# Attention in three blocks an element in place of six, between the products of an MLP mixer

## The chip, the cores and the metric

One core of one Trainium2 chip runs the whole program. The metric is device time in microseconds (us) of one execution; the kernel before took 1268.9 us (median of three runs, 1266.23 to 1271.95).

## The reference

Attention over normalised queries and keys, then an MLP mixer on its output, all in float32. There are 8 elements (batch), 12 heads, 448 positions and 64 numbers a head; the mixer has a width of 768, 256 token features and 1536 channel features.

```
q_n, k_n = rmsnorm(q) * g_q, rmsnorm(k) * g_k        # over the 64 numbers of a head
scores = q_n @ k_n.T / sqrt(64)                      # 448 x 448 for each head
attn   = exp(scores - max); attn /= sum(attn) + 1e-9
x      = (attn @ v), heads side by side              # 8 x 448 x 768
u      = x + (relu(x.T @ w_tok1) @ w_tok2).T         # mixing over positions
out    = u + relu(u @ w_ch1) @ w_ch2                 # mixing over channels
```

## The kernel before, in words

Everything is laid out by hand: within `manual_schedule` each engine runs its instructions in the order in which Python issues them, and semaphores hold an instruction until its operands and its buffer are ready. SP issues nearly all DMAs, also in that order.

**Heads and pairs.** Two heads make a pair `p` (48 in all, six an element), two pairs make a step `t` (24 in all, three an element). Attention of a step consists of seven scores (`score(t, k)`, L459: four quarter-array matmuls of 64x64 weights against 448 columns, then two exponentials on ACT, L463, into a tile `e`), seven value columns (`values(pair, k)`, L532, into the two banks `o_ps` of `ps_O`), the sums of the seven `e` tiles on DVE (`group_sums`, L500, six adds into `es`), and `row_sums` (L512), which multiplies `es` by ones into two tiles `d_ps`. `denominators` then takes for each pair the transpose of `d_ps` on DVE (L561) and its reciprocal (L563), in `begin`, and in `end` the transposed reciprocal (L575) and the product with `o_ps` (L578) into `uT`, the attention's output.

**Norms.** The queries and keys of a pair are squared on ACT (`square`, into the one tile `sq`), reduced on DVE (`reduce`, L1549), folded by four small copies on ACT (L1557), rooted by a first guess on DVE (L1571) and three Newton steps of four instructions on POOL (L1579 to L1582), scaled on DVE (`scale`, L1600) and transposed on DVE (`turn_qk`, L436), with a scaling on ACT for one of the two (L439). Only then can the pair's scores be taken. The next pairs' q and k are loaded into the same two tiles afterwards (L1514).

**Mixing.** Elements are mixed one after the other while attention is taken one element ahead. For an element `b` from 2 on the mixing is: `tok1` (L850, L857); `tok2` (L977), or for elements 3 to 6 the seven products of `seven_items` (L936); sums of the moving operand (`moving_sums`, L998 to L1002); 21 products of `ch1` (three groups of seven, L1097, twelve matmuls as the profile counts them), whose results are combined through `r` tiles by ACT, DVE and POOL (L1103, L1107, L1119) into `hb`; and 15 products of `ch2` in two halves each (L1163, eight matmuls a half), combined by L1178. Both halves of a `ch2` product go into one PSUM bank, as do the two halves of one output of `plain_2`, which stands for `ch2` in element 1. Further sums within `hb` (`x_form`, L1137) make the operands of the next `ch2` products.

**PSUM.** The eight banks are split: `ps_S` has four (scores, `d_ps`, some `tok1`), `ps_O` two, `ps_M` two (`m_tile()`: all the mixing's products). A tile gets a bank of its pool that is free by then, and its first matmul waits for the bank's last reader.

**Blocks.** From step `BIG` (9) on, a step's attention matmuls are issued in two blocks: `first_block` (scores 0 and 1, the step before's last values, its row sums, score 2) and `second_block` (scores 3 and 4, values 0 to 3, scores 5 and 6). `BLOCKS` names the places of the six blocks of an element among its mixing products (0 to 20 are `ch1`, 21 to 50 the halves of `ch2`), and `place` puts each block there and spreads the DVE, ACT and POOL items that belong behind it (`between`) evenly over the products up to the next block. Element 1 has one block, the first half of step 9, put by `merge` among `plain_2`.

Of the kernel before, what the change touches and what calls it, by code (L numbers as in the profile page):

```python
# [83 lines left out]
def whole(ctx, tc, shifted, pre, q, k, v, g_q, g_k, moe_w_tok1, moe_w_tok2, moe_w_ch1, moe_w_ch2, out):  # L84


    nc = tc.nc
# [10 lines left out]
    NPAIR = H // 2  # L98
# [15 lines left out]
    NM = S // P  # L114
    assert S - NM * P == D and NM == NS - 1 and NJ == 2

    UNITS = 8
    WCOLS = 512

# [287 lines left out]

    def load_v(p):
        b, hs = heads(p)
        st["v", p] = vt = pre.v_0 if p == 0 else st["v45"][:, p - 4, :] if p in (4, 5) else pre.v_t[p % 3]  # L410
# [129 lines left out]
    def row_sums(t):  # L540
        es = st.pop(("es", t))
        for p in (2 * t, 2 * t + 1):
            st["d", p] = s_tile("d_ps")
            ones(p, es[:, p % 2, :], start=True, stop=True)

    def denominators(ps):

        def begin(p):
            b, j = divmod(p, NPAIR)
            if j == 0:  # L550
                st["uT", b] = uT_pool.tile([P, NC, S], F32, name="uT")
# [9 lines left out]
            nc.vector.transpose(out=dt[:], in_=src)  # L561
            st["rc", p] = rc = pre.nt_pool.tile([P, NB], F32, name="rc")
            nc.vector.reciprocal(out=rc[:], in_=dt[:].rearrange("p (n c) -> p n c", c=32)[:, :, 0])  # L563

        def raw(p):

            b, j = divmod(p, NPAIR)
            to = st["uT", b][:, j, :]
            nc.scalar.copy(out=to, in_=st["o", p][:, 0:S])
            st["o", p] = to  # L570

        def end(p):
            b, j = divmod(p, NPAIR)
# [12 lines left out]
    BIG = NPAIR + NPAIR // 2  # L586

    def big_step(t, second):

        p, n = 2 * t, 2 * t + 2  # L590
        pair, last, live, more = (p, p + 1), (p - 2, p - 1), p < NP, 2 * t + 2 < NP
        item = lambda fn, *a, c=0.4: (c, lambda: fn(*a))
        loads = lambda j: [(0.3, fn) for fn in pre.loads(j, st, nc.sync, nc.sync)] if j < NP else []

        def first_block():
            if live:
                score(t, 0)
                score(t, 1)
            if more and t > BIG:
                pre.reduce(n, st)  # L600
                pre.square(n + 1, st)
            for k in range(NK - 2 - (t > BIG), NK):
# [4 lines left out]
            if live:  # L607
                score(t, 2)

        def second_block():  # L610
            score(t, 3)
            score(t, 4)
            for k in range(4):
                values(pair, k)
            score(t, 5)
            score(t, 6)
            for i in pair:
                st.pop(("qkT", i))

        if not second:  # L620
            squares = [item(fn, i, st) for i in (n, n + 1) for fn in (pre.square, pre.reduce)] if more else []
            ahead, beside = (squares[:1], squares[3:]) if t > BIG else ([], [])
            between = [item(group_sums, t, k) for k in (1, 2) if live]
            ends, roots = ([(0.4, fn) for fn in fns] for fns in (denominators(last), pre.roots(n, st) if more else []))
            if t == BIG:
                return ahead, (5.4, first_block), beside, between + ends + [
                    item(load_v, i, c=0.0) for i in pair] + squares + roots
            between += roots[:1] + ends[:2] + roots[1:2]
            between += [it for both in zip(ends[2:], roots[2:4]) for it in both] if more else ends[2:]
            between += roots[4:] + [item(load_v, i, c=0.0) for i in pair if live]  # L630
            return ahead, (5.4, first_block), beside, between
        beside = [item(scale, n), item(scale, n + 1), item(turn_qk, n, 1), item(turn_qk, n, 0)] if more else []
        beside += [item(group_sums, t, k) for k in (3, 4)]
        between = [item(turn_qk, n + 1, 1), item(turn_qk, n + 1, 0)] + loads(n + 2) if more else []
        between += [item(group_sums, t, k) for k in (5, 6)] + loads(n + 3)
        return [], (6.2, second_block), beside, between

    def place(units, blocks, at, later_beside):

        res, i, rest = [], 0, []  # L640
        for j, (ahead, block, beside, between) in list(zip(at, blocks)) + [(len(units), ([], None, [], []))]:
            n, done = j - i, 0
            for m in range(n):
                if m == n - 1 and block:
                    res += ahead
                res.append(units[i + m])
                upto = -(-len(rest) * (m + 1) // n)
                res += rest[done:upto]
                done = upto
            if not n:  # L650
                res += rest + ahead
            i, rest = j, between
            if block and later_beside and not j - at[0]:
                res.append(block)
                rest = beside + between
            elif block:
                res += [block] + beside
        return res

    def att_step(g):  # L660
# [95 lines left out]
            items.append((0.0, lambda: load_v(p + 1)))  # L756
        if live and s == 1 and 5 < p + 2 < NP:
            items.append((0.0, lambda: load_v(p + 2)))
        js = []
        if live and s == 0:  # L760
            js = [n, n + 1] if pre.plain(p) else [n + 1]
# [466 lines left out]
    def x_items(b, h):  # L1228
        return [(0.1, lambda j=j: trans_x(b, j)) for j in range(h * NC // 2, (h + 1) * NC // 2)]
# [113 lines left out]
    left, (some, sums) = [], sum_items()  # L1343
    for b in range(B):
        early, double = middle_items(b)
        if b == 0:
# [21 lines left out]
        att = []  # L1368
        if b + AHEAD < B and (shifted or b < 2):
            att = att_items(lo, lo + 10) + x_items(b + AHEAD, 0)  # L1370
            if shifted:
                att += att_items(lo + 10, lo + per)
            elif not b:
                step = att_step(lo + per - 1)
                att += att_items(lo + 10, lo + per - 1) + step[:5] + x_items(1, 1) + step[5:]
            else:
                run(att[:6])
                ahead, block, beside, between = big_step(BIG, False)
                att = att[6:] + att_items(lo + 10, lo + per - 1) + ahead + [block] + beside + between
        elif b + AHEAD < B:  # L1380
            t = (b + AHEAD) * NPAIR // 2
            blocks = [big_step(t + i // 2, i % 2) for i in range(1, NPAIR + 1)]
            blocks[4][3].extend(x_items(b + 1, 0))
            early = place(early, blocks, [near(early, at) for at in BLOCKS], in_seven(b))
        if b == 0:
            last = x_items(1, 1) * shifted + merge(last, sums[:5], turns(b, y_order(b)[2:4]))
        else:
            if b + 1 < B:
                last = merge(last, x_items(b + 1, 1))
            if b == 2 and not shifted:  # L1390
                last.append((0.4, right_sums))
            last += last_items(b, ends)
# [279 lines left out]
```

## Time and profile before

| | |
|---|---|
| runs, median (lowest to highest) | 1268.9 us (1266.23 to 1271.95) |
| profiled execution, its own time | 1268.99 us |
| its span | 1267.2 us |
| granted TensorE clock | 1.0 |
| busy: PE, PEld, DVE, ACT, POOL | 98%, 71%, 65%, 31%, 34% |
| one element of the steady part (3 to 6) | 146.90 us |
| DVE, ACT, POOL busy in such an element | 98.8, 46.2, 44.7 us |

PE is TensorE's matmuls, PEld its weight loads, DVE VectorE, ACT ScalarE, POOL GpSimd, SP the DMA-issuing engine. A line of a timeline gives start, duration, engine, source line, operation, output and inputs, shapes and the number of merged instructions; matmuls are pipelined, so the difference of two starts says what a stretch cost, and the duration is a little longer. A line of the groups gives the number of instructions after the x, then the busy time in us, the mean of one in ns and the idle time before them with what ended it. Each float32 matmul of the program is two in the profile.

### The profile page before, as it was taken

How to read it: one execution, taken by the hardware profiler on the slowest of the kernel's cores; microseconds unless marked ns; L12 is line 12 of the kernel's file. 1: busy time of each engine (PE TensorE's matmuls, PEld its weight loads, DVE VectorE, ACT ScalarE, POOL GpSimd, SP SyncE). 2: the span in 40 equal slices, each digit the busy share in tenths (PEclk: the TensorE clock that was granted, in tenths of full speed). 3: DMA queues.
4: the chain of work that ended last, by engine and by line, in shares of the span. 5: the costliest groups of instructions: out<-in, count | busy, mean ns of one | idle time of the engine just before them, and what ended most of it. 6: DMA issues, size and time to landing. Idle time of an engine off the chain costs nothing.

```text
span 1267.2 us, 20382 instructions
## 1 busy us (share of the span) xinstructions
PE 1244.7 (98%) x7322; PEld 903.5 (71%) x7322; DVE 827.8 (65%) x1293; ACT 397.1 (31%) x797; POOL 434.0 (34%) x674
## 2 busy tenths in 40 slices
PE   6999999999999999999999999999999999999998
PEld 3444444457745488798778877897787878797998
DVE  6988889756663455867677476766758486554243
ACT  6664433124330134402442143312343034300210
POOL 2311641044994912234224132244122342131222
PEclk9999999999999999999999999999999999999999
DMA  9666696899889786695758757684866865386554
GB/s 210 153 172 178 189 245 177 198 251 261 223 225 265 157 202 157 142 243 110 177 145 209 164 148 179 153 224 108 193 165 144 225 131 153 117 212 144 182 174 105
DMA packets 480274, 228.39 MB, mean 180 GB/s; under 512 B 362900, under 2 KB 440084, under 8 KB 480164
## 3 DMA queue, kind: packets, MB, share of 16 engines
q1 hardware_dynamic: 472626, 211.85, 66.9%
q0 software_dynamic: 4512, 14.46, 4.0%
q8 instruction: 60, 0.98, 0.3%
q10 hardware_dynamic: 3026, 0.69, 0.3%
q14 instruction: 50, 0.41, 0.1%
HBM read 184.26 MB, written 42.66 MB: 179 GB/s over the span
## 4 chain that ended last, share of the span: by engine, by line
PE 86%; DVE 5%; SPq 3%; DMA 2%; issue 1%; ACT 1%; POOL 1%; DVEq 0%; ACTq 0%; POOLq 0%
PE m_ps L1097 26%; PE m_ps L1163 22%; PE s_ps L459 10%; PE o_ps L532 9%; PE m_ps L1067 5%; PE m_ps L977 3%; PE m_ps L850 3%; PE t_ps L850 2%; PE m_ps L1146 1%; PE seven_ps L936 1%; PE d_ps L512 1%; PE m_ps L936 1%; PE m_ps L512 1%; DVE es L500 1%; DMA xs<-xt 1%
## 5 line engine op out<-in xcount | busy, mean ns | idle before, releaser
L1163 PEld LDWEIGHTS m_ps<-hb,unit 128*128 128x128 f32 x1440 | 270.9, 190 | 8.8 <-issue 7.7
L1163 PE MATMUL m_ps<-hb,unit 128*128 128x224 f32 x1440 | 277.2, 354 | 0.0
L1097 PE MATMUL m_ps<-tu,unit 128*128 128x224 f32 x1008 | 201.6, 355 | 1.3 <-ACT r L1107 1.3
L1097 PEld LDWEIGHTS m_ps<-tu,unit 128*128 128x128 f32 x1008 | 189.1, 190 | 15.0 <-issue 9.2
L463 ACT ACTIVATE e<-s_ps 128x448 f32<-128x448 f32 x294 | 138.3, 549 | 149.6 <-PE s_ps L459 148.9
L1097 PE MATMUL m_ps<-uT,unit 128*128 128x224 f32 x756 | 151.2, 354 | 0.6 <-DVE hb L1103 0.6
L1097 PEld LDWEIGHTS m_ps<-uT,unit 128*128 128x128 f32 x756 | 142.2, 190 | 7.7 <-POOL tu L1001 2.8
L459 PE MATMUL s_ps<-qkT 64*64 64x448 f32 x1260 | 144.3, 545 | 0.8 <-ACT x L832 0.8
L532 PE MATMUL o_ps<-e,v 64*64 64x448 f32 x1148 | 130.0, 538 | 0.0
L500 DVE TENSOR_TENSOR es<-es,e 128x896 f32<-128x896 f32 x90 | 102.9, 1143 | 11.0 <-ACT e L463 6.4
L1103 POOL TENSOR_TENSOR hb<-r,r 128x448 f32<-128x448 f32 x21 | 23.8, 1133 | 217.5 <-ACT r L1119 217.5
L1103 DVE TENSOR_TENSOR hb<-m_ps,r 128x448 f32<-128x448 f32 x63 | 39.1, 620 | 88.9 <-POOL r L1103 57.5
L459 PEld LDWEIGHTS s_ps<-qkT 64*64 64x64 f32 x1260 | 45.7, 132 | 67.9 <-issue 56.2
L1579 POOL TENSOR_TENSOR nt<-rs 128x56 f32<-128x56 f32 (+1 forms) x54 | 21.2, 393 | 201.8 <-DVE rs L1571 199.0
L532 PEld LDWEIGHTS o_ps<-e,v 64*64 64x64 f32 x1148 | 46.1, 133 | 61.9 <-issue 59.8
L1178 POOL TENSOR_TENSOR uT<-uT,r 128x448 f32<-128x448 f32 x42 | 51.4, 1241 | 78.2 <-DVE r L1178 46.6
L1104 ACT ACTIVATE hb<-hb 128x448 f32<-128x448 f32 x84 | 48.2, 575 | 90.5 <-DVE hb L1103 68.5
L1549 DVE TENSOR_REDUCE ms<-sq 128x28 f32<-128x896 f32 (+2 forms) x44 | 47.4, 1080 | 43.5 <-ACT sq L1536 36.3
L324 POOL TENSOR_TENSOR raw<-raw 128x128 f32<-128x128 f32 x128 | 65.4, 531 | 20.8 <-DMA raw<-wp 16.3
L1103 DVE TENSOR_TENSOR r<-m_ps,r 128x448 f32<-128x448 f32 x42 | 26.0, 618 | 55.2 <-PE m_ps L1097 55.2
L1174 ACT COPY r<-m_ps 128x448 f32<-128x448 f32 x24 | 12.8, 532 | 156.5 <-PE m_ps L1163 156.5
L1178 DVE TENSOR_TENSOR uT<-uT,m_ps 128x448 f32<-128x448 f32 x41 | 24.9, 619 | 54.8 <-PE m_ps L1163 54.8
(177 smaller groups left out, 1776.1 us busy)
## 6 DMA issues: line engine op xcount, KB each, us to landing
unit<-ws SPq DMA_DIRECT2D x267, 384.0 KB, 4.1
raw<-in_moe_w_ch_dram SPq DMA_DIRECT2D x72, 256.0 KB, 3.6
v<-in_v_dram SPq DMA_DIRECT2D x96, 112.0 KB, 3.6
out_dram<-turned SPq DMA_DIRECT2D x182, 56.0 KB, 2.0
xs<-xt SPq DMA_DIRECT2D x52, 168.0 KB, 4.5
qk_t<-in_q_dram SPq DMA_DIRECT2D x144, 56.0 KB, 3.5
qk_t<-in_k_dram SPq DMA_DIRECT2D x144, 56.0 KB, 3.4
x<-xs SPq DMA_DIRECT2D x39, 192.0 KB, 4.2
```

The costliest lines, as they stand in the source:

```text
L324: nc.gpsimd.tensor_tensor(out=at[o], in0=at[x], in1=at[y], op=ALU.add if op == "+" else ALU.subtract)
L459: nc.tensor.matmul(out=pss[i][rows_of(i, a), 0:S], lhsT=qkT[h, 1, k * D:(k + 1) * D], rhs=qkT[h, 0, :], start=True, stop=True)
L463: nc.scalar.activation(out=e[:, i, :], in_=pss[i][:, 0:S], func=AF.Exp)
L500: nc.vector.tensor_tensor(out=es[:], in0=(es if k > 1 else st["e", t, 0])[:], in1=st["e", t, k][:], op=ALU.add)
L532: nc.tensor.matmul(out=st["o", p][a * D:(a + 1) * D, 0:S], lhsT=vt[rows, k * D:(k + 1) * D], rhs=e[rows, :], **kw)
L850: nc.tensor.matmul(out=st["t1", h][jc][:, 0:HC], lhsT=w1_sb[:, c, jc * P:(jc + 1) * P], rhs=st["x", b, h][:, :, c, :], start=start and c = ...
L1067: nc.tensor.matmul(out=ps, lhsT=a[:, o + 2 * half, :], rhs=natural(half * KF + t) if wide else u[:, half * KC + t, :], start=(t == 0 and h ...
L1097: nc.tensor.matmul(out=ps[:, j * HS:(j + 1) * HS], lhsT=w[:, t, j, :], rhs=m, start=(t == 0), stop=(t == KC - 1))
L1103: add = lambda e, o, x, y: e.tensor_tensor(out=o, in0=x, in1=y, op=ALU.add)
L1104: relu = lambda name: put_off(lambda: nc.scalar.activation(out=h[name], in_=h[name], func=AF.Relu))
L1163: nc.tensor.matmul(out=ps[:, x * HS:(x + 1) * HS], lhsT=st["w"][:, tile_at % 6, :], rhs=hb[:, X_SLOT[f], i, :], start=(i == 0), stop=(i == 3))
L1178: e.tensor_tensor(out=get(out), in0=get(x_), in1=get(y), op=ALU.add if op == "+" else ALU.subtract)
```

## The change

Each step from 9 on has one block in place of two, and an element three in place of six. The block holds scores 0 and 1, the step before's last two value columns, its row sums, the first half of its endings (`begin` on DVE and, new for these pairs, a copy of `o_ps` to `uT` on ACT), and then a score and a value column in turn, with the group sums between them. `row_sums` takes its two tiles from `ps_M` in place of `ps_S`. Behind each block come the rest of the endings, the value loads, and the whole of the next pairs' norms, spread over the products up to the next block; behind an element's last block `norms` are spread over what is left of `early`, and `turned` is merged with the transposes of x in `last`. Four value tiles are used in turn, so that a step's two tiles can be loaded while the last step's are in use.

```
+    BIG = NPAIR + NPAIR // 2
 def load_v(p):
+        if p >= 2 * BIG and not shifted:
+            vt = (pre.v_0, pre.v_t[0])[p % 2] if p // 2 % 2 else pre.v_t[1 + p % 2]
 def row_sums(t):
-            st["d", p] = s_tile("d_ps")
+            st["d", p] = m_tile() if t >= BIG - 1 else s_tile("d_ps")
 def denominators(ps):
-        if ps[0] < NPAIR:
+        if ps[0] < NPAIR or ps[0] >= 2 * BIG - 2 and not shifted:
             parts += [lambda p=p: raw(p) for p in ps]
-    def big_step(t, second):
+    def big_step(t):
...
+        def block():
+            if live:
+                score(t, 0)
+                score(t, 1)
+            for k in (NK - 2, NK - 1):
                 values(last, k)
             row_sums(t - 1)
             for i in last:
                 st.pop(("v", i))
+            for part in ends[:4]:
+                part()
+            if not live:
+                return
+            group_sums(t, 1)
+            score(t, 2)
+            for k in range(3, NK):
+                values(pair, k - 3)
+                group_sums(t, k - 1)
+                score(t, k)
+            values(pair, NK - 3)
...
+        beside = [item(group_sums, t, NK - 1)] if live else []
+        ends_ = [(0.4, fn) for fn in ends[4:]]
+        if not more:
+            return (11.3 if live else 2.3, block), beside, ends_, [], []
+        norms = [item(fn, i, st) for i in (n, n + 1) for fn in (pre.square, pre.reduce)]
+        norms += [(0.4, fn) for fn in pre.roots(n, st)] + [nothing] * 4
+        turned = [item(scale, n), nothing, item(scale, n + 1), nothing, item(turn_qk, n, 1), item(turn_qk, n, 0)] + loads(n + 2)
+        turned += [item(turn_qk, n + 1, 1), item(turn_qk, n + 1, 0)] + loads(n + 3)
+        values_in = [item(load_v, i, c=0.0) for i in (n, n + 1)]
+        return (11.3, block), beside, ends_ + values_in, norms, turned
...
-    BLOCKS = (0, 6, 11, 17, 23, 31)
+    BLOCKS = (0, 14, 28)
...
+                block, beside, ends_, norms, turned = big_step(BIG)
+                att = att[6:] + att_items(lo + 10, lo + per - 1) + [block] + beside + ends_
+                carry = [(0.4, lambda: None)] * 14 + norms + turned
         elif b + AHEAD < B:
             t = (b + AHEAD) * NPAIR // 2
-            blocks = [big_step(t + i // 2, i % 2) for i in range(1, NPAIR + 1)]
-            blocks[4][3].extend(x_items(b + 1, 0))
-            early = place(early, blocks, [near(early, at) for at in BLOCKS], in_seven(b))
+            steps = [big_step(t + i) for i in range(1, NPAIR // 2 + 1)]
+            blocks = [(block, beside, ends_ + norms + turned) for block, beside, ends_, norms, turned in steps[:2]]
+            blocks[1][2].extend(x_items(b + 1, 0))
+            block, beside, ends_, norms, turned = steps[2]
+            blocks.append((block, beside, ends_ + norms))
+            early = place(early, blocks, [near(early, at) for at in ((8, 20, 30) if b == 2 else BLOCKS)], carry)
+            behind, carry = turned, []
...
-                last = merge(last, x_items(b + 1, 1))
+                last = merge(last, x_items(b + 1, 1) + behind)
```

More of the change, by code (lines that the diff above doesn't have):

```diff
@@ L409, in load_v @@
         b, hs = heads(p)
-        st["v", p] = vt = pre.v_0 if p == 0 else st["v45"][:, p - 4, :] if p in (4, 5) else pre.v_t[p % 3]
+        if p >= 2 * BIG and not shifted:
+            vt = (pre.v_0, pre.v_t[0])[p % 2] if p // 2 % 2 else pre.v_t[1 + p % 2]
+        else:
+            vt = pre.v_0 if p == 0 else st["v45"][:, p - 4, :] if p in (4, 5) else pre.v_t[p % 3]
+        st["v", p] = vt
         for a in range(2):
@@ L585, in whole @@
     NG = 2 * NP
-    BIG = NPAIR + NPAIR // 2
-    def big_step(t, second):
+    assert BIG % 2
+    def big_step(t):
         p, n = 2 * t, 2 * t + 2
@@ L592, in big_step, with some @@
         item = lambda fn, *a, c=0.4: (c, lambda: fn(*a))
-        loads = lambda j: [(0.3, fn) for fn in pre.loads(j, st, nc.sync, nc.sync)] if j < NP else []
-        def first_block():
+        nothing = (0.4, lambda: None)
+        loads = lambda j: [item(some, j, lo) for lo in (0, 4)] if j < NP else []
+        ends = denominators(last)
+        def some(j, lo):
+            for fn in pre.loads(j, st, nc.sync, nc.sync)[lo:lo + 4]:
+                fn()
+        def block():
             if live:
@@ L598, in first_block @@
                 score(t, 1)
[L599 to L602, printed above, removed]
+            for k in (NK - 2, NK - 1):
                 values(last, k)
@@ L606, in first_block @@
                 st.pop(("v", i))
[L607 to L616, printed above, removed]
+            for part in ends[:4]:
[8 more added lines that the diff above has]
+                score(t, k)
@@ L617, in second_block @@
+            values(pair, NK - 3)
             for i in pair:
                 st.pop(("qkT", i))
[L620 to L641, printed above, removed]
+        beside = [item(group_sums, t, NK - 1)] if live else []
@@ L642, in place @@
+        values_in = [item(load_v, i, c=0.0) for i in (n, n + 1)]
+        return (11.3, block), beside, ends_ + values_in, norms, turned
+    def place(units, blocks, at, rest):
+        res, i = [], 0
+        for j, (block, beside, between) in list(zip(at, blocks)) + [(len(units), (None, [], []))]:
             n, done = j - i, 0
             for m in range(n):
-                if m == n - 1 and block:
-                    res += ahead
                 res.append(units[i + m])
@@ L650, in place @@
             if not n:
-                res += rest + ahead
+                res += rest
             i, rest = j, between
[L653 to L656, printed above, removed]
+            if block:
                 res += [block] + beside
@@ L758, in att_step @@
             items.append((0.0, lambda: load_v(p + 2)))
+            if t == BIG - 1 and not shifted:
+                items.append((0.0, lambda: load_v(p + 3)))
         js = []
@@ L1342, in whole @@
         att_items(0, 8) + merge(att_items(8, AHEAD * per + 1), x_items(0, 0)), weight_items(0, BEFORE)))
-    left, (some, sums) = [], sum_items()
+    left, carry, (some, sums) = [], [], sum_items()
     for b in range(B):
@@ L1367, in whole @@
         lo = (b + AHEAD) * per + 1
-        att = []
+        att, behind = [], []
         if b + AHEAD < B and (shifted or b < 2):
@@ L1377, in whole @@
                 run(att[:6])
-                ahead, block, beside, between = big_step(BIG, False)
-                att = att[6:] + att_items(lo + 10, lo + per - 1) + ahead + [block] + beside + between
+                block, beside, ends_, norms, turned = big_step(BIG)
+                att = att[6:] + att_items(lo + 10, lo + per - 1) + [block] + beside + ends_
+                carry = [(0.4, lambda: None)] * 14 + norms + turned
         elif b + AHEAD < B:
             t = (b + AHEAD) * NPAIR // 2
-            blocks = [big_step(t + i // 2, i % 2) for i in range(1, NPAIR + 1)]
-            blocks[4][3].extend(x_items(b + 1, 0))
-            early = place(early, blocks, [near(early, at) for at in BLOCKS], in_seven(b))
+            steps = [big_step(t + i) for i in range(1, NPAIR // 2 + 1)]
[5 more added lines that the diff above has]
+            behind, carry = turned, []
         if b == 0:
```

## The prediction

> **What bounds the kernel now.** I read the page first, then PE's timeline over one element, then every engine's timeline where mixing passes from its first to its second product stage, then the groups by shape.
>
> ```profile
> PE 1244.7 (98%) x7322; PEld 903.5 (71%) x7322; DVE 827.8 (65%) x1293; ACT 397.1 (31%) x797; POOL 434.0 (34%) x674
> PE 86%; DVE 5%; SPq 3%; DMA 2%; issue 1%; ACT 1%; POOL 1%; DVEq 0%; ACTq 0%; POOLq 0%
> ```
>
> PE is the bound; the chain of waits is PE for 86%. In the steady part (elements 3 to 6, each 146.90 us by the windows) PE never stands still, so a change gains by taking work or gaps off PE, and loses whatever it makes PE wait. DVE is busy 98.8 us of each 146.9: enough room in total, but its queue is in order.
>
> ```profile
> 798.49 2.43 PE L1097 MATMUL m_ps<-tu,unit 128*128 128x224 f32 x12
> 800.76 3.19 PE L1163 MATMUL m_ps<-hb,unit 128*128 128x224 f32 x16
> 803.88 1.74 PE L459 MATMUL s_ps<-qkT 64*64 64x448 f32 x16
> 805.43 2.44 PE L532 MATMUL o_ps<-e,v 64*64 64x448 f32 x24
> 807.69 0.93 PE L532 MATMUL o_ps<-cv_sb,v 64*64 64x448 f32 x8
> 808.44 1.68 PE L459 MATMUL s_ps<-qkT 64*64 64x448 f32 x16
> 810.05 12.37 PE L1163 MATMUL m_ps<-hb,unit 128*128 128x224 f32 x64
> 822.36 1.73 PE L459 MATMUL s_ps<-qkT 64*64 64x448 f32 x16
> 826.17 0.93 PE L512 MATMUL d_ps<-es,one_c 64*64 64x448 f32 x8
> 826.92 0.93 PE L459 MATMUL s_ps<-qkT 64*64 64x448 f32 x8
> ```
>
> Differences of starts are the true costs. Four quarter-array matmuls go together in 0.376 us (24 values: 807.69 - 805.43 = 2.26 for six groups); two row sums take 0.75. A mixing matmul takes 0.189 (twelve in 800.76 - 798.49). So a ch1 product (12) is 2.27, a ch2 half (8) is 1.51. What lies above that is the price of a block: 16 mixing matmuls before it take 3.12 instead of 3.03, the block of 16 groups 6.17 instead of 6.02, and the 64 after it 12.31 instead of 12.11, 0.09 of which belong to the next entry. That is 0.09 + 0.15 + 0.11 = 0.35, call it 0.36 us a block.
>
> ```profile
> 796.22 2.43 PE L1097 MATMUL m_ps<-uT,unit 128*128 128x224 f32 x12
> 796.47 0.53 ACT L1119 COPY r<-m_ps 128x448 f32<-128x448 f32 x1 [2.80 <-PE m_ps L1097]
> 797.08 1.13 POOL L1103 TENSOR_TENSOR hb<-r,r 128x448 f32<-128x448 f32 x1 [17.23 <-ACT r L1119]
> 798.18 1.13 POOL L1103 TENSOR_TENSOR r<-r,r 128x448 f32<-128x448 f32 x1
> 799.34 0.62 DVE L1103 TENSOR_TENSOR hb<-m_ps,r 128x448 f32<-128x448 f32 x1 [0.76 <-POOL r L1103]
> ```
>
> The fifth ch1 product ends at 796.22; the sixth product's add on DVE, which needs its sum, ends at 799.97, 3.75 later. What stands behind that add on DVE starts no sooner.
>
> ```profile
> L561 DVE STREAM_TRANSPOSE dt<-d_ps 128x448 f32<-128x448 f32 x42 | 26.0, 618 | 5.4 <-PE d_ps L512 5.4
> L1600 DVE TENSOR_TENSOR qk_t<-qk_t,rs 128x896 f32<-128x896 f32 x36 | 46.5, 1332 | 5.9 <-POOL rs L1582 2.9 <-DMA unit<-ws 2.9
> L436 DVE STREAM_TRANSPOSE qkT<-qk_t 128x448 f32<-128x448 f32 x72 | 42.0, 618 | 1.4 <-PE s_ps L459 1.4
> L439 ACT ACTIVATE qkT<-qkT,g_t 128x448 f32<-128x448 f32 x36 | 24.3, 675 | 66.4 <-DVE qkT L436 66.3
> ```
>
> **Blocks: a gain.** Before, 31 blocks (one in element 1, six in each of 2 to 6); after, 1 + 5 x 3 = 16. The matmuls are the same. 15 x 0.36 = -5.4 us, all on PE.
>
> Inside a long block (11.3 us) I walked the engines. Per step PE needs 1.50 (a score and a value column), ACT two exponentials at 0.44 from start to start, 0.9; the two new o_ps copies (0.54 each) end some 0.3 before the next values need the banks; five e buffers come round in time, since the first group sum ends near 6.9 and the sixth score's exponential starts near 9.3. So nothing inside a block costs PE time, but DVE leaves it with a group sum still to do, 1.5 us into the mixing.
>
> **Row sums in the mixing's banks: a loss.** ps_M has two banks. The block of element 1 and the last block of each of elements 2 to 6 (at 28 or 30 among the mixing's products) stand between the two halves of one output: ch2 counts from 21, so 28 and 30 are odd halves; in element 1, five of plain_2's halves precede it. One bank is then half written and held, so both row sums go through the other. The order of the changed program shows it: in these six places the second row sum's matmuls wait for DVE's transpose of the first, and everything behind them on PE waits too. First row sum alone: 0.38 to its second pass, 0.54 to its end (536 ns a matmul, by the view of tile d_ps), 0.62 for the transpose (L561), 0.1 for two hand-offs (799.31 to 799.34 is one): the second starts 1.64 later than beside the first. 6 x 1.64 = +9.8. Bounds: the transpose and hand-offs alone, 0.72, or 4.3 in all; a row sum not overlapped with anything more, 2.4, or 14.4. I take 1.64, since no row lets a second row sum start sooner. In the other ten blocks both banks are free and nothing waits.
>
> **Norms behind the blocks.** Squares, reductions, roots, scales and transposes of the next pairs now all stand between one block and the next; before, they were spread over two gaps and the block between.
>
> *Second blocks of elements 3 to 6.* The last two transposes of the next pairs stand behind the sixth product's add. From the fifth product's end: 3.75, two transposes 1.16, ACT's scaling 0.68: 5.6. PE reaches the block two products later, at 4.6: late by 1.0. 4 x 0.95 = +3.8 (bounds 0 and 6).
>
> *Third blocks of elements 3 to 5*, 26.5 us after the second. DVE from the block's end: group sum to 1.5, a form (L1137, 1.0) to 2.4, two endings (2.4) to 4.9, adds of products 2 and 3 as they come to 7.6, form 8.6, reduction 9.6. sq is one tile, so the second square waits for that: ACT to 10.7, reduction 11.8, four halves on ACT to 12.9. Only then comes ACT's copy of the fifth product (ready at 11.5): its two POOL adds end at 15.7, DVE's add at 16.4, and the first ch2 product, ready at 15.9, waits 0.5 for that bank. POOL's three root steps (4.4) end at 20.1, the scales (2 x 1.33) at 22.7, two transposes, two forms, an add and two transposes at 27.6, ACT at 28.3; PE is there at 27.1 and waits 1.2. Together 1.7.
> One row makes it worse:
>
> ```profile
> 805.64 1.15 POOL L1178 TENSOR_TENSOR uT<-uT,r 128x448 f32<-128x448 f32 x1
> 805.72 3.02 DVE L1600 TENSOR_TENSOR qk_t<-qk_t,rs 128x896 f32<-128x896 f32 x2 [1.44 <-DMA unit<-ws]
> ```
>
> With a POOL add beside it the pair of scales takes 3.02, not 2.6, and such an add falls on the first scale here: 0.4 more, 2.1 in all, x 3 = +6.3 (bounds 0 and 9). [...]
>
> *Third block of element 2*: only one ch1 product and nine halves (15.9 us) lie before it. Roots start near 10, end near 14.5; scales to 17; the add that frees the tenth half's bank follows at 17.7, where PE was ready at 14.7; then transposes and ACT to 20.6 against 19.2. +4.4 (bounds 0 and 7).
>
> *After the third blocks* DVE owes endings, two reductions, forms and transposes for the norms among ch2's adds. Walked the same way, the fourth and sixth adds after the block come 0.6 too late for their banks: 1.2 for elements 3 to 5, 1.5 for element 2 with its four halves left: +5.1 (bounds 0 and 9).
>
> **Rest, at nothing:** q, k and v loads keep their number and issue on SP behind transposes; they are needed a whole gap later, and weights run some 16 us (seven units) ahead, so SP may stand for that long. The o_ps copies are on ACT (31% busy). If that cover went, each copy would cost PE 0.54.
>
> **Sum.** -5.4 + 9.8 + 3.8 + 6.3 + 4.4 + 5.1 = +24.0 on the profiled execution's 1268.99, which equals the runs' median of 1268.9: 1293.0.
>
> **Rivals.**
> A (0.70): the sum, 1280 to 1306.
> B (0.14): the norms fit; items are early enough or rows that I took at their means run shorter side by side. For it: DVE has 48 us free an element. Against it: the order is fixed and the last transposes stand behind a late add. Only the row sums stay: 1269.0 - 5.4 + 9.8 = 1273.4.
> C (0.08), not slower: the 0.36 decides. The row sums' wait must be hidden in the third block's own start and the norms' too; then 1269.0 - 5.4 = 1263.6. It decides if waits per element stay under 3 x 0.36 = 1.1 us; one bank for two row sums speaks against it.
> D (0.08): DVE's lag carries from gap to gap and becomes the bound: the norms' 19.6 twice, 1312.6.
>
> **Numbers.** This kernel's measurement can tell about 0.5% (6.3 us) from no change. Range 1273 (B's end) to 1307 (A's sum, row sums at their upper 14.4, norms half as much again: 1293.0 + 4.6 + 9.8). Faster than 1262.6 needs more than C gives: 0.03. Within 0.5%: C and most of B, 0.16. Slower: 0.81.
>
> **What would show it.** Right: six row-sum pairs with about 1.6 us between first and second, and a DVE transpose inside; PE idle before the scores of second and third blocks, released by ACT's qkT; L1163 matmuls waiting for DVE after third blocks; 16 blocks at the same 0.36. Wrong: row sums back to back in third blocks, or PE gapless there.

## The result, and the profile after

Over six timed executions of each kernel on one chip the changed kernel takes 1324.5 us (median) against 1268.8 us; the ratio is 1.043, 95% interval 1.041 to 1.045. The forecast was 1293.0 us with a range of 1273 to 1307: the direction was right, the size was not, and the time lies 17 us above the range. The profiled execution took 1320.5 us, with a span of 1318.6 against 1267.2.

The page of the changed kernel, engines and chain of waits:

```profile
PE 1261.2 (96%) x7322; PEld 910.2 (69%) x7322; DVE 830.6 (63%) x1293; ACT 422.9 (32%) x829; POOL 440.1 (33%) x674
PE 75%; DVE 9%; DMA 4%; SPq 3%; POOL 3%; issue 3%; ACT 2%; DVEq 0%; ACTq 0%; POOLq 0%
```

The same 7322 matmuls now keep PE busy 16.5 us longer, although there are half as many blocks. Part of that is a lower clock: some of them ran at half the clock (0.50 granted), for 17 us in all, which makes at most 8.5 us; that is not a wait and stands in no list of waits. Another part is matmuls that overlap less: where one pair of a block comes late, its quarter-array matmuls go two at a time and not four. At 654.04, in the second block of element 3, two start, at 654.47 two more and from 655.01 on four together; to the next mixing matmul PE is busy for 12.39 us without a gap, where the first block of that element (610.62) takes 11.45. PE carries 75% of the chain, not 86%: DVE has 4 points more, DMA and POOL 2 each.

What PE waits for in the changed kernel (us in total, number of times, longest). Left out are a wait of 9.4 us at the start (10.0 in the kernel before) and, but for the last row, those of 1.6 us and less:

```profile
PE m_ps L1163 <- DMA unit<-ws: 10.0, 4, 3.2
...
PE m_ps L1163 <- DVE r L1178: 8.4, 8, 1.7
PE m_ps L1163 <- DVE uT L1178: 5.6, 1, 5.6
PE m_ps L517 <- DVE dt L566: 4.8, 6, 0.9
PE m_ps L1163 <- DVE ms L1571: 3.6, 1, 3.6
...
PE s_ps L464 <- ACT qkT L444: 1.0, 2, 0.6
```

(L517, L464, L1163 and L1097 of the changed kernel are the row sums, the scores, and the products of the second and of the first multiplication; L566 is the transpose of a row sum, L444 ACT's scaling of a transpose, L441 the transposes of q and k, L1605 their scales, L1519 their loads.) The rows from the second on are waits of the kinds that the prediction named. The first is not: four times the product's weights were not there, once in each of elements 2 to 5. The third and the fifth row are one wait each, and both lie in element 2, right ahead of its third block and behind it. (For the fifth the profile names a step of the norms' roots on DVE; the addition L1178 just ahead of it on DVE, at 561.28, is the one that reads the product's bank.)

PE's timeline, one such wait from each row but the last:

```profile
533.61 3.36 PE L1163 MATMUL m_ps<-hb,unit 128*128 128x224 f32 x8 [5.59 <-DVE uT L1178]
562.04 7.97 PE L1163 MATMUL m_ps<-hb,unit 128*128 128x224 f32 x32 [3.56 <-DVE ms L1571]
699.73 0.59 PE L517 MATMUL m_ps<-es,one_c 64*64 64x448 f32 x2 [0.83 <-DVE dt L566]
727.09 16.16 PE L1163 MATMUL m_ps<-hb,unit 128*128 128x224 f32 x84 [1.72 <-DVE r L1178]
745.20 3.73 PE L1163 MATMUL m_ps<-hb,unit 128*128 128x224 f32 x12 [1.96 <-DMA unit<-ws]
```

The first and the last of these show the second loss as well. Eight matmuls at 533.61 take 3.36 us and twelve at 745.20 take 3.73, where the trace of before has twelve in 2.43. The trace grants half the clock from 531.3 for 6.8 us, and from 562.1, 746.4 and 1057.0 for 3.4 us each. In the kernel before there is no such stretch between 14 and 1266 us.

Why the weights are late shows in SP's queue at the end of element 3:

```profile
727.61 1.88 SPq L1519 DMA_DIRECT2D qk_t<-in_q_dram  x4
729.59 0.42 SPq L1025 DMA_DIRECT2D unit<-ws  x1
...
730.53 3.13 SPq L1519 DMA_DIRECT2D qk_t<-in_k_dram  x4
733.76 1.99 SPq L1519 DMA_DIRECT2D qk_t<-in_q_dram  x4
735.85 0.42 SPq L1025 DMA_DIRECT2D unit<-ws  x1
...
739.15 2.17 SPq L1519 DMA_DIRECT2D qk_t<-in_k_dram  x4
741.42 3.71 SPq L1025 DMA_DIRECT2D unit<-ws  x7
```

Sixteen loads of q and k, about half a microsecond of issue each where they come without a gap, stand between the unit loads, with sends and loads of x among them; ahead of the first SP stands 3.6 us for DVE's transposes (`SPq L1519 <- DVE qkT L441`). From 727.6 to 741.4 two units are issued; then seven come at once, and the product that wants the first of them at 743.2 goes at 745.20. That unit was issued at 741.42 and landed at 745.16, 3.7 us later, where the median of these loads is 3.4: it was late in SP's queue, not in the transfer.

Lengths of the elements, from the first matmul of a token stage to that of the next, in us more than before. The forecast's own terms give the first column, with half a block (6.2 us of PE) that the change moves from element 6 to element 1:

| | forecast | changed | e1_loads | e5_loads_element2 | e10_second_pair_later |
|---|---|---|---|---|---|
| element 1 | +7.8 | +7.9 | +10.9 | +12.6 | +5.9 |
| element 2 | +6.4 | +19.4 | +16.3 | +2.4 | +0.4 |
| elements 3, 4, 5 | +4.8 each | +8.9, +8.5, +10.1 | +5.0 each | +5.0 each | +2.8, +2.8, +3.1 |
| element 6 | -4.7 | -4.0 | -4.0 | -3.9 | -4.9 |
| span | +24.0 | +51.4 | +40.8 | +28.9 | +10.2 |

### The profile page after: what moved, and what is told of

It reads as the page before. It is cut to its first block, busy times and chain, and to the rows that moved or that the text cites. A ratio compares the mean times of both kernels' runs of the same rounds, so it can differ in the third digit from the quotient of the medians.

```text
span 1318.6 us, 20485 instructions
## 1 busy us (share of the span) xinstructions
PE 1261.2 (96%) x7322; PEld 910.2 (69%) x7322; DVE 830.6 (63%) x1293; ACT 422.9 (32%) x829; POOL 440.1 (33%) x674
## 4 chain that ended last, share of the span: by engine, by line
PE 75%; DVE 9%; DMA 4%; SPq 3%; POOL 3%; issue 3%; ACT 2%; DVEq 0%; ACTq 0%; POOLq 0%
PE m_ps L1097 21%; PE m_ps L1163 12%; PE s_ps L464 9%; PE o_ps L537 9%; PE m_ps L1067 6%; PE m_ps L1146 4%; PE m_ps L850 3%; PE t_ps L850 2%; DMA unit<-ws 2%; PE m_ps L977 2%; PE m_ps L517 2%; PE seven_ps L936 1%; DVE ms L1554 1%; PE m_ps L936 1%; SPq L1519 1%
## 5 line engine op out<-in xcount | busy, mean ns | idle before, releaser
L1163 PE MATMUL m_ps<-hb,unit 128*128 128x224 f32 x1440 | 285.8, 359 | 28.6 <-DMA unit<-ws 10.0
L1163 PEld LDWEIGHTS m_ps<-hb,unit 128*128 128x128 f32 x1440 | 274.7, 193 | 40.5 <-DMA unit<-ws 11.6
L1097 PE MATMUL m_ps<-tu,unit 128*128 128x224 f32 x1008 | 199.1, 353 | 2.7 <-POOL tu L1002 1.4
L1097 PEld LDWEIGHTS m_ps<-tu,unit 128*128 128x128 f32 x1008 | 190.0, 190 | 8.3 <-issue 2.8
L464 PE MATMUL s_ps<-qkT 64*64 64x448 f32 x1260 | 183.4, 546 | 2.1 <-ACT qkT L444 1.0
L468 ACT ACTIVATE e<-s_ps 128x448 f32<-128x448 f32 x294 | 144.9, 550 | 110.2 <-PE s_ps L464 106.1
L1097 PE MATMUL m_ps<-uT,unit 128*128 128x224 f32 x756 | 152.0, 354 | 0.7 <-DVE uT L982 0.6
L1097 PEld LDWEIGHTS m_ps<-uT,unit 128*128 128x128 f32 x756 | 141.9, 190 | 10.3 <-issue 3.9
L537 PE MATMUL o_ps<-e,v 64*64 64x448 f32 x972 | 148.5, 538 | 0.0
L1103 POOL TENSOR_TENSOR hb<-r,r 128x448 f32<-128x448 f32 x21 | 24.9, 1186 | 275.1 <-ACT r L1119 274.6
L464 PEld LDWEIGHTS s_ps<-qkT 64*64 64x64 f32 x1260 | 59.1, 133 | 78.0 <-issue 60.0
L1178 POOL TENSOR_TENSOR uT<-uT,r 128x448 f32<-128x448 f32 x42 | 52.2, 1255 | 162.2 <-DVE r L1178 112.7
L1103 DVE TENSOR_TENSOR hb<-m_ps,r 128x448 f32<-128x448 f32 x63 | 39.1, 620 | 103.6 <-POOL r L1103 60.6
L537 PEld LDWEIGHTS o_ps<-e,v 64*64 64x64 f32 x972 | 49.3, 133 | 54.1 <-issue 51.4
L1104 ACT ACTIVATE hb<-hb 128x448 f32<-128x448 f32 x84 | 48.4, 576 | 107.5 <-DVE hb L1103 79.1
L444 ACT ACTIVATE qkT<-qkT,g_t 128x448 f32<-128x448 f32 x36 | 24.1, 669 | 150.0 <-DVE qkT L441 150.0
L1605 DVE TENSOR_TENSOR qk_t<-qk_t,rs 128x896 f32<-128x896 f32 (+1 forms) x42 | 57.1, 1385 | 21.7 <-POOL rs L1587 17.8
L1178 DVE TENSOR_TENSOR uT<-uT,m_ps 128x448 f32<-128x448 f32 x41 | 24.5, 611 | 58.8 <-PE m_ps L1163 58.8
L1554 DVE TENSOR_REDUCE ms<-sq 128x28 f32<-128x896 f32 (+2 forms) x44 | 47.5, 1082 | 17.6 <-ACT sq L1541 10.6
## 6 DMA issues: line engine op xcount, KB each, us to landing
raw<-in_moe_w_ch_dram SPq DMA_DIRECT2D x72, 256.0 KB, 3.5
```

Source lines behind the costliest of these rows:

```text
L464: nc.tensor.matmul(out=pss[i][rows_of(i, a), 0:S], lhsT=qkT[h, 1, k * D:(k + 1) * D], rhs=qkT[h, 0, :], start=True, stop=True)
L468: nc.scalar.activation(out=e[:, i, :], in_=pss[i][:, 0:S], func=AF.Exp)
L537: nc.tensor.matmul(out=st["o", p][a * D:(a + 1) * D, 0:S], lhsT=vt[rows, k * D:(k + 1) * D], rhs=e[rows, :], **kw)
L1097: nc.tensor.matmul(out=ps[:, j * HS:(j + 1) * HS], lhsT=w[:, t, j, :], rhs=m, start=(t == 0), stop=(t == KC - 1))
L1103: add = lambda e, o, x, y: e.tensor_tensor(out=o, in0=x, in1=y, op=ALU.add)
L1163: nc.tensor.matmul(out=ps[:, x * HS:(x + 1) * HS], lhsT=st["w"][:, tile_at % 6, :], rhs=hb[:, X_SLOT[f], i, :], start=(i == 0), stop=(i == 3))
```

## The experiments

All ratios are to the kernel before, run beside it; that of the changed kernel is 1.043.

**e1_loads**: the last step's loads go into the next element's token stage.

```diff
-            behind, carry = turned, []
+            behind, carry = turned[:6] + turned[8:10], turned[6:8] + turned[10:]
```

> The changed kernel with one edit: the q and k loads behind an element's third block (16 DMAs in SP's queue, beside the element's last products) are issued in the next element's token stage, ahead of its first block; the scales and transposes stay where they are. Theory L: SP stands behind these loads and the mixing weights come late; the waits of PE for units (10.0 us in the profile of the changed kernel, at the end of elements 2 to 5) and the two stretches of half clock that follow them at 746 and 1057 us (some 1.7 us each) go, so 11 to 14 us less than 1324.5: about 1312. Rival R1: the weights are only late because PE's products were already held by DVE, whose lag then comes to the fore: at most 4 us less, 1320 to 1324, with the wait for the unit turned into one for DVE. Rival R2: the loads are as costly in the token stage, where sends and x loads use the queue too: 1322 to 1332, with new waits for x or weights there.

Measured: 1306.0 us, ratio 1.027 (1.023 to 1.030), so 20.8 us less by the ratios, with the two intervals 16 to 26. The list of waits has no unit any more, and neither half-clock stretch at the end of elements 3 and 5 is left (mean clock 0.996 for 0.993); elements 2 to 5 are 3.1, 3.9, 3.4 and 5.1 us shorter, 15.5 together. Theory L holds, a little larger than stated. (The spans of the two profiled executions differ by 10.6 us only: elements 0 and 1, which come ahead of the edit, took 3.9 us more in this one.) With the weights in time, the same product behind the third block still waits for DVE:

```profile
728.02 18.43 PE L1163 MATMUL m_ps<-hb,unit 128*128 128x224 f32 x96 [1.19 <-DVE r L1178]
```

but by 1.19 and not 1.72 us, and the 96 matmuls behind it run to the end of the element without a break: R1 (the wait becomes one for DVE) and R2 are out.

**e2_sums_in_s**: the row sums go back to the score banks.

```diff
-            st["d", p] = m_tile() if t >= BIG - 1 else s_tile("d_ps")
+            st["d", p] = s_tile("d_ps")
```

> The changed kernel with one part undone: the row sums of a block lie in the four score banks again, not in the two banks of the mixing. Theory S: in each of the six blocks the second pair's sums no longer wait for the transpose of the first out of the one free bank, 1.73 us in the profile of the changed kernel for each, so 10.4 us less: about 1314. Rival: the score that follows in the block then waits for a score bank in its place, as the sums hold two of the four until the transposes have read them: within 3 us of 1324.5, the wait moved from the second sums to the next scores. If anything else of the 55 us came by way of these banks (products that wait for the bank behind a block), more than 14 us go.

Measured: 1326.8 us, ratio 1.046 (1.040 to 1.052): nothing gained. The waits for the second sums are gone, and the third blocks of elements 3 to 5 fall from 13.85 to 12.77 us (from the first start to the last end, as all lengths of blocks here). But the first blocks of elements 3 to 6 rise from 11.73 to 14.4, by this wait in PE's timeline:

```profile
617.14 1.37 PE L464 MATMUL s_ps<-qkT 64*64 64x448 f32 x6 [1.67 <-DVE dt L566]
```

There the transposes come late on DVE, and until they have read the sums, two of the four score banks are held. The rival is right. The 1.0 us that a pair of sums waits in the mixing's banks is real, but it isn't a loss against the other place for them in this schedule.

**e3_element2**: element 2 as the others.

```diff
-                att = ... + [block] + beside + ends_
-                carry = [(0.4, lambda: None)] * 14 + norms + turned
+                att = ... + [block] + beside + ends_ + norms + turned
-            ... near(early, at) for at in ((8, 20, 30) if b == 2 else BLOCKS)
+            ... near(early, at) for at in BLOCKS
```

> The changed kernel with element 2 arranged as the others: its blocks stand at products 0, 14 and 28 (not 8, 20 and 30), and the norms and transposes of the pairs of the block in element 1 stay behind that block in element 1 (not carried into element 2's token stage and first eight products). Theory P: element 2 is 19.4 us longer than before because the first block has moved off the token stage, where it covered the sums for the products, and because the third stands so late that the norms run into the end of the element; with this edit it loses as much as elements 3 to 5 do (about 9 us), so about 10 us less: 1314. Rival: element 2 is long because it has two sets of norms in it and no place of the blocks matters; with one set back in element 1, that element gets the longer by the same: within 3 us of 1324.5.

Measured: 1317.9 us, ratio 1.036 (1.032 to 1.040), 9 us less than the changed kernel by the ratios. Element 2 loses 13.1 us and element 1 takes 5.5 more. Theory P holds for element 2; the rival has its part in element 1. The edit moves the blocks and the norms together, so what each of the two is worth is not shown.

**e4_before_sums_in_m**: the kernel before, with the row sums of 15 blocks in the mixing's banks and their transposes inside the block.

```diff
+            st["d", p] = m_tile() if t >= BIG else s_tile("d_ps")
...
+            if t > BIG:
+                for part in denominators(last)[:2]:
+                    part()
...
-            between += roots[:1] + ends[:2] + roots[1:2]
+            between += roots[:2]
```

> The kernel before with one part alone: the row sums of the first blocks of elements 2 to 6 (15 blocks) lie in the two banks of the mixing, and the transposes that empty them are issued inside the block, as in the changed kernel; the blocks stay six an element, at places where no product is open across them. Theory S: with no product open, the two sums have a bank each but the second must wait until the product ahead of the block has been evicted: 0 to 0.6 us each, so 1269 to 1278. Rival: the cost of 1.7 us belongs to the banks and not to the place: 15 times 1.7 is 26 us, about 1294.

Measured: 1270.4 us, ratio 0.9998 (0.998 to 1.002). At these places, where no product is open, the half block with the sums takes 5.76 us for 5.71, and the other 6.46 as before. By itself, this part of the change costs nothing that can be measured.

**e5_loads_element2**: e1 and e3 together.

> Both earlier edits in one kernel: the q and k loads of the third block's step in the next element's token stage, and element 2 arranged as elements 3 to 5 (its norms behind element 1's block, blocks at 0, 14 and 28). Theory (two causes that add up): elements 2 to 5 all take the 151.9 us that elements 3 to 5 took with the loads moved, so 14.9 us less than that kernel's 1308.0 us span in element 2, some 2.5 us more in element 1: a ratio to the kernel before of 1.015 to 1.020, no stretch of half clock between 20 us and the end but possibly one in element 1, and no wait for a unit. Rival: the two edits save the same microseconds, as late weights were a part of what element 2 lost: ratio 1.024 or more.

Measured: 1298.0 us, ratio 1.021 (1.019 to 1.024). The two causes add up, nearly to the stated 1.015 to 1.020; element 1 took 1.7 us more than in e1 and not the 2.5 stated, and element 2 took 152.9 us. Both together are 27 us of the changed kernel's 55. Two stretches of half clock are left, at 212.8 us in element 0 and at 322.0 us in element 1 (mean clock 0.997).

**e6_clean_third**: e5 with `BLOCKS = (0, 14, 27)`.

> As e5_loads_element2, and the third block one product half sooner (27 for 28), where no product is open across it. Theory of the place: the two row sums find a bank each, as in the kernel before with its sums in these banks, where the half block with the sums took 5.76 us against 5.71; the third block falls from 13.84 to between 11.8 and 12.8 us in elements 2 to 5, and the products behind it have one half more to cover the norms: 4 to 9 us less than e5_loads_element2. Rival, the banks themselves: the second pair's sums wait wherever the block stands, since the bank of the product ahead is still being emptied: within 2 us of e5_loads_element2.

Measured: 1300.4 us, ratio 1.023 (1.020 to 1.026), no different from e5. The third block stays at 13.74 us. The waits of PE show that the theory of the place was right about the sums and wrong about the time: of the six waits for L517 one is left (0.8 us, in element 1), and in their stead stands

```profile
PE s_ps L464 <- ACT qkT L444: 5.3, 6, 1.1
```

With the block 1.5 us earlier, its scores come before their transposes: what the sums no longer wait, the scores wait more. The rival's number came out, but not its reason.

**e7_clean_early**: e6, and the items behind a block end two products ahead of the next one.

```diff
-                upto = -(-len(rest) * (m + 1) // n)
+                upto = -(-len(rest) * min(m + 1, max(1, n - 2)) // max(1, n - 2))
```

> As e6_clean_third, and the norms, scales and transposes behind a block are spread so that the last of them stands two products ahead of the next block instead of right before it. Theory of the lag: the second and third blocks start their scores on transposes that have only just been issued; with two products (3 to 4.5 us) between, their waits for qkT go (0.95 us in the second block of elements 2 to 5, 0.3 to 0.7 in the third): 4 to 7 us less than e6_clean_third. Rival: DVE works through the same list closer packed, so it falls behind on the sums that empty the products' banks, and what the blocks win the products lose: within 2 us, or slower.

Measured: 1293.8 us, ratio 1.018 (1.016 to 1.021), 6 us less than e6. Every second and third block of elements 2 to 5 now takes 11.72 us: all their waits are gone. Against that the products pay more than before:

```profile
PE m_ps L1163 <- DVE r L1178: 13.1, 8, 1.8
```

(5.7 us in e6, with 4.5 more for `uT` of the same line.) So the theory and its rival both hold, the first with the larger part.

**e8_spaced**: e7 with `BLOCKS = (0, 13, 25)`.

> As e7_clean_early, with the blocks at 0, 13 and 25 instead of 0, 14 and 27: nine halves and not seven between the third block and the end of the spread, 13 products and not 14 between the first and second. Theory: after the third block DVE's lag shows as 1.5 us at one product; with two more halves behind it that wait shrinks by about 1 us in elements 2 to 5, so 2 to 5 us less than e7_clean_early. Rival: the lack of room moves ahead, to the stretch between the second and the third block, where DVE has x forms as well: 0 to 5 us more. In no theory does it come below the kernel before, since the first block of element 1 and the last of element 6 keep their 5 to 9 us: ratio 1.000 to 1.012.

Measured: 1315.4 us, ratio 1.035 (1.033 to 1.037): 22 us slower than e7, far beyond the rival's 5. POOL and DVE ahead of the first product of the second multiplication, and that product:

```profile
673.60 2.08 POOL L1137 TENSOR_TENSOR hb<-hb 128x896 f32<-128x896 f32 x1
675.63 1.97 POOL L1103 TENSOR_TENSOR hb<-r,r 128x448 f32<-128x448 f32 x1
677.57 1.97 POOL L1103 TENSOR_TENSOR r<-r,r 128x448 f32<-128x448 f32 x1
673.67 2.95 DVE L1604 TENSOR_TENSOR qk_t<-qk_t,rs 128x896 f32<-128x896 f32 x1 [3.26 <-POOL rs L1586]
676.55 2.01 DVE L1604 TENSOR_TENSOR qk_t<-qk_t,rs 128x896 f32<-128x896 f32 x1
679.57 0.62 DVE L1103 TENSOR_TENSOR hb<-m_ps,r 128x448 f32<-128x448 f32 x1 [1.02 <-POOL r L1103]
680.25 8.68 PE L1163 MATMUL m_ps<-hb,unit 128*128 128x224 f32 x32 [4.24 <-DVE hb L1103]
```

(L1604 of this kernel are the scales, L1586 the last of a Newton step.) From 668.50 to 673.6 POOL works off the norms' twelve Newton operations, and a form and the product's two sums stand behind them in its queue. Then POOL's instructions and DVE's scales, started side by side, end in turn: the first scale ends 0.95 us after the form, the first sum 0.98 after that scale, the second scale 0.95 after that sum, the second sum 0.98 after that scale. So a sum that takes 1.13 us alone (798.18 in the trace of before) takes 1.97, and the scales, 1.08 each alone (643.41 in the changed kernel), take 2.95 and 2.01. DVE's eviction waits for the sum, PE for the eviction, and half the clock for 6.8 us follows in each of elements 2 to 5 (mean clock of the run 0.989).

**e9_element1**: e7 with two weights of the spreading changed.

```diff
-                upto = -(-len(rest) * min(m + 1, max(1, n - 2)) // max(1, n - 2))
+                few = max(1, n - 2) if block else n
+                upto = -(-len(rest) * min(m + 1, few) // few)
...
-                att = ... + [block] + beside + ends_ + norms + turned
+                att = ... + [(5.4, block[1])] + [(0.2, fn) for _, fn in beside + ends_ + norms + turned]
```

> As e7_clean_early, with two weights of the spreading changed: in element 1 the block counts as half as long and the norms behind it as half as much, so that the attention ahead of it is spread as in the kernel before; and behind the third block the norms use the whole stretch up to its end again. Theory: in e7_clean_early element 1 takes 178.9 us, where the kernel before takes 163.0 and the half block moved into it 6.2; the difference of 9.7 us is DVE behind early in the element (a wait of 3.9 us and 6.8 us at half clock at 320 us), and goes to less than 4; the waits of 1.8 and 1.6 us behind the third block shrink to 1.3 each: 6 to 11 us less than e7_clean_early, a ratio to the kernel before of 1.010 to 1.014. Rival: the norms in element 1 cost DVE's time wherever they stand, now at its end: within 3 us of e7_clean_early.

Measured: 1285.8 us, ratio 1.011 (1.007 to 1.015). Element 1 falls from 178.9 to 172.4 us, and its stretch at half clock is gone (mean clock 1.0, where e7 has 0.997). The theory holds.

**e10_second_pair_later**: e9 with

```diff
-            behind, carry = turned[:6] + turned[8:10], turned[6:8] + turned[10:]
+            behind, carry = turned[:6], turned[6:]
```

> As e9_element1, and the transposes of the last step's second pair (four DVE and ACT operations an element) go into the next element's token stage with its loads, so that DVE has some 5 us less to do beside an element's last products. Theory: the wait of about 1.3 us at the product ten halves before the end of elements 2 to 5 goes or halves: 2 to 5 us less than e9_element1, ratio 1.006 to 1.012, still not below the kernel before. Rival: the token stage has no room on DVE, which makes its sums for the products there: the first block or the first products wait instead, 0 to 6 us more than e9_element1.

Measured: 1282.8 us, ratio 1.010 (1.006 to 1.014), within the theory's range, but no different from e9 by the intervals. In the profile the wait ten halves before the end is gone from elements 3 to 5, which are 0.4 to 0.7 us shorter.

**e11_second_sooner**: e10 with `BLOCKS = (0, 12, 27)`.

> As e10_second_pair_later, with the second block two products sooner (12 for 14). In e10 the first product of the second multiplication waits 1.0 us for DVE, which stands 5.2 us for a sum that POOL makes only after eight short instructions of the Newton steps of the norms (655.7 to 658.5 us). Theory of the norms' place: two products sooner, the Newton steps fall on other sums; the wait at the first product of the second multiplication goes, or moves to a product of the first multiplication: 1279 to 1284, within 4 us of e10. Rival: as at 13 in e8_spaced, DVE's scale then waits for these steps in front of an eviction, 4 us and a stretch of half clock an element: 15 to 25 us more than e10. In neither does it come below the kernel before.

Measured: 1295.6 us, ratio 1.020 (1.018 to 1.022), 13 us slower than e10 and between the two theories: the eviction does come late, by 2.25 us and not by 4. The case is worth more for the clock. PE's timeline in element 3 and in element 4, and then a stretch of 8 us around each of these waits by the windows (busy us of PE, weight loads, DVE, ACT and POOL, the granted clock, the DMA share and GB/s); element 2 is like 3, and 5 like 4 (L1164 and L1104 of this kernel are L1163 and L1103 of the changed one):

```profile
665.62 9.35 PE L1164 MATMUL m_ps<-hb,unit 128*128 128x224 f32 x48 [2.23 <-DVE hb L1104]
817.62 11.03 PE L1164 MATMUL m_ps<-hb,unit 128*128 128x224 f32 x48 [2.23 <-DVE hb L1104]
```

```profile
664.70:672.70 8.00, 7.08 (x37) 7.08 (x38) 7.28 (x11) 2.71 (x5) 1.57 (x2) 1.00 0.38 85
816.70:824.70 8.00, 7.08 (x28) 6.76 (x29) 6.82 (x10) 2.82 (x5) 1.34 (x2) 0.79 0.37 85
```

The same wait of 2.23 us for the same releaser costs nothing more in elements 2 and 3. In elements 4 and 5 half the clock for 3.4 us follows (0.79 on the mean of the 8): the same 48 matmuls take 11.03 us for 9.35, and the elements are 1.6 us longer (153.7 against 152.1).

No arrangement of three blocks that was run comes below the kernel before; the best, e10, is 0.6 to 1.4% slower. What is left of it is 2.9 us in each of elements 3 to 5, of which two waits show some 2: the first product of the second multiplication for DVE (1.0) and a product behind the third block for DVE (1.1).

## Why the prediction was wrong, step by step

**"Rest, at nothing" is the step that failed first.** It counted the loads of q and k and found their number unchanged, and let SP stand for 16 us because the weights run seven units ahead. But the change puts all sixteen loads of the third step beside the last dozen product halves of an element, behind a wait for DVE and with x sends and loads between them, and there SP issues two units in 14 us while PE uses one about every 2.3 us (twelve matmuls of 0.19 us as the profile counts them). The lead is eaten up: the unit issued at 722.59 is some 14 us ahead of its product, the one issued at 741.42 is 1.8 us ahead. The trace of before showed the issue time of such a load and the order of SP's queue was known; the sum of the two was not made. e1 prices the step at 15.5 us by the elements and about 21 (16 to 26) by the times, where the prediction had 0.

**The clock is a term that the sum lacked.** The trace of before grants full clock from 14 to 1266 us, so nothing in it says what a wait costs beyond itself; the wait alone, a bound from below, was taken for the whole price. In the changed kernel 17 us ran at half clock, at most 8.5 us lost, which the prices of the loads and of element 2 partly contain.

**Element 2 was mis-sized.** The sum had 4.4 + 1.5 us for its third block and 1.6 for the row sums. It measured +19.4. The waits right before and behind the third block alone are 5.6, 3.6 and 1.1 us (the walk had PE ready 3.0 us ahead of the first, and 1.5 for those behind), plus two stretches of half clock (6.8 and 3.4 us, from 531.3 and 562.1); and the first block's move from the token stage to the eighth product, which uncovers the sums for the first products (waits of 0.4 and 1.4 us at 442 and 451 us), was not costed at all. e3 shows the price of the arrangement, its places and its norms together: 13.1 us in the element, 9 net.

**What was walked through came out.** With the two failed stretches mended, e5 runs at 1298.0 us against the forecast's 1293.0, and elements 3 to 5 take 5.0 us more than before where the terms gave 4.8. Singly: six pairs of row sums do wait, 1.0 us on PE's steps (1.37 instead of 0.38) where the term had 1.64; second blocks of elements 3 to 5 are late by 12.67 - 11.73 = 0.94 (forecast 0.95), that of element 6 by 1.6; in elements 3 to 5 the first product of the second multiplication waits 0.3 (0.5), and the product behind the third block 1.2 in e1 (1.2). That the sums agree so well is partly luck: in e1 a product right ahead of the third block waits 0.7 us, which no term names, while the third block's scores are late by 12.77 - 11.73 = 1.04 (in e2, where no sums wait) and not 1.6, and the row sums cost 0.6 less. And as e6 and e7 show, the waits inside the blocks and those at the products behind them trade against each other.

**Blocks: right.** From the start of the tenth mixing matmul ahead of a block to that of the eleventh behind it, undisturbed, the two short blocks before take 9.40 and 10.16 us and a long one (in e7) 15.42. The difference of 4.14 holds twenty more mixing matmuls (3.78), which leaves 0.36 for the block that is saved, as forecast: 5.4 us in all.

**Row sums: right wait, too large a charge.** The second sums start 1.75 us after the first (699.73 and 697.98), near the 1.64. But PE fills part of that with matmuls of other groups, so its steps lose 1.0: about 6 us in the six places, where the term had 9.8. The place makes the wait (an open product): where none is open, sums in the same banks cost nothing, as the half block of 5.76 us in e4 and the long ones of 11.72 in e7 show. e2 shows that with the sums back in the score banks the scores of other blocks wait in their stead.

**Rivals.** B fails: the norms did not fit. C fails: waits of some 5 us an element stand against 3 x 0.36. D, at 1312.6, was the nearest in size and named the wrong cause: what carried the time beyond A was SP's queue, element 2 and the clock. The row that the prediction used for the scales beside a POOL add held: in the changed kernel the pair takes 3.01 us (722.96). The first of the two, which takes 1.08 alone, takes 2.01 there; it starts just behind a POOL sum of 1.13 (722.89) and ends 0.95 after that sum. But the 2.6 for a pair without such a sum was a mean that contains these delays: a pair alone takes 2.08 (766.81 in the trace of before).

## What to carry to other kernels

When a change moves work in order, walk every queue that issues, SP's too, over the stretch where it becomes densest, and set what it issues there against what PE uses up there; a lead of some microseconds in buffers says nothing until this sum is made. A wait on an otherwise full PE can have a second price: of the changed kernel's four waits for late weights (3.17, 1.96, 2.14 and 2.73 us) the second and the fourth were followed by 3.4 us at half the clock, at most 1.7 us lost each. And when one wait is removed, look for the one that comes in its place: in e6 and e2 the time stayed the same although the wait that was aimed at had gone.

## What the runs showed of the hardware

**The granted clock.** Between 12.5 and 1316.4 us the trace of the changed kernel grants in turn full and half clock, for 518.8, 6.8, 23.9, 3.4, 180.9, 3.4, 307.2, 3.4 and 256.0 us: 152, 2, 7, 1, 53, 1, 90, 1 and 75 times 3.413 us. Cut this stretch into pieces of 3.413 us and add up PE's idle time in each. Ahead of the program's last products, the pieces at full clock with most of it were those from 558.65, 527.93 and 1053.58 (3.39, 3.32 and 2.60 us), and half the clock followed on each. Of the two with 1.96 us it followed on the one from 742.97 and not on the one from 585.96; it followed on none with less (the next in size, from 899.98, has 1.76). So of the waits for late weights those of 1.96 us (743.24) and 2.73 us (1054.40) were followed by half the clock. That of 2.14 us (899.61) was not, and neither was that of 3.17 us (587.41), which lies in two pieces with 1.96 and 1.20. The twelve matmuls behind the waits of 1.96 and 2.73 us took 3.73 and 4.14 us, those behind the wait of 2.14 took 2.54; in e11 the 48 behind the wait of 2.23 took 1.68 us more at half clock for 3.4 us. Whether it is the idle time in such pieces that decides was not tried by an experiment of its own.

**POOL and DVE held each other up in both directions.** In e8 POOL's sums of 1.13 us took 1.97 and DVE's scales of 1.08 us took 2.95 and 2.01 where they were started side by side: each ended 0.95 to 0.98 us after the other engine's. The prediction had counted such a loss for DVE alone, and for a single sum.
